# Two attention and feed-forward layers on one core: five more chunks transposed by VectorE and a trip through DRAM

## The chip, the cores and the metric

The kernel runs on one core of a Trainium2 chip. Time is device microseconds of one execution; the time of a kernel is the median of its runs. The core's engines each work through a queue of their own in the order in which the program issues their instructions: TensorE (PE in the profile; matrix multiplications and transposes, results in PSUM banks), VectorE (DVE), ScalarE (ACT), GpSimd (POOL) and SyncE (SP), whose queue issues nearly all DMA transfers. An instruction waits, with everything behind it on its engine, until what it reads has been written and what it overwrites has been read.

## The reference

`x` is 2048 rows of 448 numbers in float32. Two layers follow each other, with the same weights: attention with 16 query heads of 28 and one shared key and value head, and a gated feed-forward of width 1792, each behind a normalization of the rows and added to `x`:

```python
q = (x @ wq).reshape(B, S, H, Dh).transpose(0, 2, 1, 3)
k, v = x @ wk, x @ wv
p = softmax(einsum("bhqd,bkd->bhqk", q, k) * Dh ** -0.5)
A = einsum("bhqk,bkd->bhqd", p, v).transpose(0, 2, 1, 3).reshape(B, S, H * Dh) @ wo
B = (silu(x @ w_gate) * (x @ w_up)) @ w_down

x = x + A(layernorm(x))
x = x + B(layernorm(x))
x = x + A(layernorm(x))
x = x + B(layernorm(x))
```

## The kernel before

The 2048 rows are four chunks (0 to 3) of 512 rows, each chunk four blocks of 128 rows. `xres` holds `x` in SBUF with rows on the partitions. A product needs the chunk the other way round, with the 448 columns on the partitions (four slabs `k` of 128, the last one of 64), and as a high part `xh` and a remainder `xl`, so that three products of reduced precision stand for one of float32.

*From rows to a chunk's `xh` and `xl`.* `norm_steps` takes the statistics of four blocks (VectorE, `stats`, `mv`), the reciprocal deviation `rstd` (GpSimd) and the normalized rows `xn` (VectorE). There are two ways on from there:

- TensorE's way: `flip` (L243) issues sixteen transposes of 128x128 into PSUM banks; `flipped` lets ScalarE copy each bank to `xh` and VectorE subtract to get `xl`. GpSimd first copies the last 64 columns of `xn` once more (`twice`), so that both halves of the last slab are filled.
- VectorE's way: `turn_tile` (L266) transposes squares of 32x32 within a block, `send` (L270) stores the result to DRAM so that the squares come to lie in the right rows, a load brings it back (into `xn`, or into two of the query buffers, `qstack`), and `halved` (L286) makes `xh` and `xl` of it. The rows of the chunk then stand in another order, which later readers undo in their access patterns (`natural`, `in_order`, for the chunks listed in `squares`).

*The projection.* `Attention.project` runs sixteen products in `order`, four to a chunk; `seen` counts them, and q0 to q15 are their names in the text. Each is 11 matmuls into one PSUM bank (L312). ScalarE copies the bank out twice (L538, L539, the second into a `stage` buffer, of which the first layer has three and the second two), SyncE stores it (`qd`, and the keys `kt`), and for the two products of a chunk that hold values VectorE transposes 32 partitions (`vt`, L546). After q6, q10 and q14 four matmuls (L438, `maxima`) bound the scores of the chunk before; VectorE transposes their result (`sg`, L440), reduces it, splits it and transposes it again (`flat`), and SyncE stores it. `plan[n, 0]` and `plan[n, 1]` are lists of work issued just ahead of and just behind product n, and `when` another list behind it.

In the first layer chunks 0 to 3 all take TensorE's way: the transposes of a chunk are issued one product ahead of its first (for chunk 1, behind q3). In the second layer the last group of the feed-forward hands each chunk over as it is finished (`hand_over`): chunks 0 to 2 take VectorE's way, chunk 3 TensorE's.

*The scores* of a layer follow q15, in 128 steps that ScalarE's exponentials and TensorE fill between them. While they run, chunks 0 to 2 of the feed-forward are turned VectorE's way.

*The feed-forward* goes through seven groups of two slices of 128 columns of the 1792; a `unit` is one slice for one chunk: 42 matmuls in two halves, with the two halves of the unit before's product with `w_down` in between and behind (L332). `soon` is a list of work issued so many units later. Chunk 3 is finished last by the attention; it takes TensorE's way, its transposes issued in two blocks in the middle of the unit ahead of its first (`mid[0, 2, 1]`, the second unit of chunk 2).

The order of instructions on every engine is the order in which these functions issue them; nothing reorders it. The whole computation stands in the program a second time, with exact maxima, behind a test that doesn't ask for it on these inputs.

## Time and profile before

| | us |
|---|---|
| median of 3 runs (lowest, highest) | 1962.88 (1962.73, 1963.62) |
| the profiled execution | 1962.25 |
| its span | 1960.4 |
| TensorE matmuls, busy | 1943.3 (99%) |
| ScalarE, busy | 1264.1 (64%) |
| VectorE, busy | 968.3 (49%) |
| GpSimd, busy | 553.6 (28%) |
| first projection, first product to first scores | 12.0 to 63.7 |
| granted TensorE clock, mean | 0.998 |

Times in the views are microseconds from the start of the span. A row of a timeline is start, length, engine, line, operation, what is written from what is read, shapes and count; in brackets stands the idle time ahead of it and who ended it. A matmul's length is from its start to its result, and neighbours overlap, so what one costs is the distance between starts.

### The profile page before, as it was taken

How to read it: one execution, taken by the hardware profiler on the slowest of the kernel's cores; microseconds unless marked ns; L12 is line 12 of the kernel's file. 1: busy time of each engine (PE TensorE's matmuls, PEld its weight loads, DVE VectorE, ACT ScalarE, POOL GpSimd, SP SyncE). 2: the span in 40 equal slices, each digit the busy share in tenths (PEclk: the TensorE clock that was granted, in tenths of full speed). 3: DMA queues.
4: the chain of work that ended last, by engine and by line, in shares of the span. 5: the costliest groups of instructions: out<-in, count | busy, mean ns of one | idle time of the engine just before them, and what ended most of it. 6: DMA issues, size and time to landing. Idle time of an engine off the chain costs nothing.

```text
span 1960.4 us, 44004 instructions
## 1 busy us (share of the span) xinstructions
PE 1943.3 (99%) x18469; PEld 1325.5 (68%) x18469; DVE 968.3 (49%) x1638; ACT 1264.1 (64%) x1888; POOL 553.6 (28%) x593
## 2 busy tenths in 40 slices
PE   9999999999999999999999999999999999999998
PEld 7544545445468999999974445454454799988886
DVE  6656575665743223223666565657656433223223
ACT  4899898998943333333349998989989333333332
POOL 4213123132214333333341221121231332323320
PEclk9999999999999999999999999999999999999999
DMA  5111011121130011110251110110211200011102
GB/s 166 55 36 29 21 40 40 29 53 43 26 87 20 17 32 32 32 29 19 67 156 34 37 30 22 50 28 24 67 40 32 71 28 21 17 32 32 32 2 77
DMA packets 100643, 83.61 MB, mean 43 GB/s; under 512 B 25080, under 2 KB 81656, under 8 KB 100440
## 3 DMA queue, kind: packets, MB, share of 16 engines
q1 hardware_dynamic: 98888, 79.55, 14.7%
q8 instruction: 145, 2.38, 0.5%
q10 hardware_dynamic: 1552, 1.20, 0.2%
q14 instruction: 58, 0.48, 0.1%
HBM read 57.38 MB, written 21.50 MB: 40 GB/s over the span
## 4 chain that ended last, share of the span: by engine, by line
PE 87%; ACT 9%; DMA 1%; DVE 1%; issue 1%; POOL 0%; SPq 0%; ACTq 0%; POOLq 0%; DVEq 0%
PE bank L332 40%; PE bank L688 20%; PE bank L633 14%; ACT pt L655 6%; PE three L633 5%; PE bank L312 4%; ACT pair L656 2%; PE three L612 2%; PE bank L612 1%; PE three L621 0%; PE bank L438 0%; DMA kt<-stage 0%; DMA xd<-xh 0%; DMA wr<-in_A_wq_dram 0%; DVE vt L546 0%
## 5 line engine op out<-in xcount | busy, mean ns | idle before, releaser
L655 ACT ACTIVATE pt<-three 128x1536 f32<-128x1536 f32 x512 | 723.0, 1484 | 52.9 <-PE three L633 52.9
L688 PE MATMUL bank<-pt,vsb 128*32 128x512 f32 x3072 | 490.8, 599 | 0.0
L688 PE MATMUL bank<-pair,vsb 128*32 128x512 f32 x1024 | 487.5, 598 | 0.6 <-ACT pair L656 0.6
L633 PE MATMUL bank<-qstack,keys 32*128 32x512 f32 x1536 | 473.1, 425 | 0.0
L332 PE MATMUL bank<-xh,wgh 64*128 64x512 f32 x1728 | 450.7, 389 | 0.0
L633 PE MATMUL three<-qstack,keys 32*128 32x512 f32 x4608 | 428.7, 408 | 0.5 <-ACT stage L539 0.3
L633 PEld LDWEIGHTS bank<-qstack,keys 32*128 32x128 f32 x1536 | 243.5, 183 | 250.0 <-issue 124.9
L654 DVE COPY pair<-bank 128x512 f32<-128x512 f32 x512 | 354.0, 691 | 95.2 <-PE bank L633 57.4
L332 PE MATMUL bank<-xh,wgl 64*128 64x512 f32 x1404 | 371.7, 391 | 0.0
L332 PE MATMUL bank<-xl,wgh 64*128 64x512 f32 x1296 | 338.1, 390 | 0.0
L332 PE MATMUL bank<-wdh,h 64*128 64x448 f32 x1792 | 334.3, 364 | 1.1 <-ACT h L1008 0.8
L1007 DVE TENSOR_TENSOR sg<-bank,sg 128x512 f32<-128x512 f32 x112 | 77.4, 691 | 502.5 <-ACT sg L1006 500.3
L656 ACT ACTIVATE pair<-pair 128x1024 f32<-128x1024 f32 x256 | 281.5, 1100 | 0.0
L332 PEld LDWEIGHTS bank<-xh,wgh 64*128 64x128 f32 x1728 | 266.3, 185 | 16.7 <-issue 1.3
L633 PEld LDWEIGHTS three<-qstack,keys 32*128 32x128 f32 x4608 | 261.5, 183 | 13.9 <-DVE xres L604 1.5
L885 POOL TENSOR_TENSOR xres<-stage,xres 128x448 f32<-128x448 f32 x108 | 127.3, 1197 | 502.5 <-ACT stage L884 502.3
L688 PEld LDWEIGHTS bank<-pt,vsb 128*32 128x32 f32 x3072 | 101.9, 109 | 246.0 <-issue 153.1
L332 PEld LDWEIGHTS bank<-wdh,h 64*128 64x128 f32 x1792 | 247.5, 184 | 14.8 <-issue 2.0
L697 DVE TENSOR_TENSOR o<-bank,o 128x512 f32<-128x512 f32 x224 | 154.9, 691 | 203.8 <-PE bank L688 203.8
L339 ACT COPY seen<-bank 128x1 f32<-128x1 f32 x664 | 81.9, 163 | 254.3 <-PE bank L332 251.2
L332 PEld LDWEIGHTS bank<-xh,wgl 64*128 64x128 f32 x1404 | 219.2, 184 | 13.8
L332 PE MATMUL bank<-wdl,h 64*128 64x448 f32 x896 | 222.2, 367 | 0.0
(145 smaller groups left out, 2095.7 us busy)
## 6 DMA issues: line engine op xcount, KB each, us to landing
o<-rd SPq DMA_DIRECT2D x32, 256.0 KB
qraw<-qd SPq DMA_DIRECT2D x128, 56.0 KB
qd<-stage SPq DMA_DIRECT2D x28, 224.0 KB
wdr<-in_B_w_down_dram SPq DMA_DIRECT2D x28, 224.0 KB
xt<-tb SPq DMA_DIRECT2D x24, 224.0 KB
wr<-in_B_w_gate_dram SPq DMA_DIRECT2D x28, 192.0 KB
wr<-in_B_w_up_dram SPq DMA_DIRECT2D x28, 192.0 KB
xn<-xt SPq DMA_DIRECT2D x6, 768.0 KB
```

The lines of the kernel that those rows point to most:

```text
L312: nc.tensor.matmul(po, a, b, start=(i == 0), stop=(i == len(seq) - 1))
L332: nc.tensor.matmul(po, a, b, start=start, stop=stop, skip_group_check=True)
L339: nc.scalar.copy(seen[:, i : i + 1], po[:, 0:1])
L612: nc.tensor.matmul(po[:, 0:D], a[:, g, P * t : P * t + P], b[:, g, :], start=False, stop=(g == NG - 1 and z == 2), skip_group_check=True,)
L633: nc.tensor.matmul(three[:, j, :] if j < 3 else one, k[js, kp, ks], q[js, part, :], start=(z == 0), stop=(z == 2), tile_position=(32 * j, 0),)
L654: copies.append(nc.vector.tensor_copy(pt1, one))
L655: es.append(nc.scalar.activation(pt, threes[y], AF.Exp, scale=SCALE))
L656: es.append(nc.scalar.activation(pair, pair, AF.Exp, scale=SCALE))
L688: nc.tensor.matmul(to[32 * j : 32 * j + 32, :], vsb[:, n % NT, :], pts[n][j], start=(y == 0), stop=(y == 1), skip_group_check=True,)
L697: f = nc.vector.tensor_tensor(accs[i][:, 0, :], to, accs[i][:, 0, :], ALU.add)
L885: nc.gpsimd.tensor_tensor(r, s, r, ALU.add)
L1007: nc.vector.tensor_tensor(in_order(sg, sq), natural(pg[1], sq), in_order(sg, sq), ALU.mult)
```

## The change

Five chunks go from TensorE's way to VectorE's: chunks 2 and 3 of the first layer's projection, chunk 3 of the second layer's, and chunk 3 of both feed-forwards. Eighty of TensorE's transposes go.

- In the first layer (`by_vector`), chunk 2's statistics are issued behind q1, its normalization and transposes behind q2, its stores behind q3, its load behind q4, and its `xh` and `xl` ahead of q7; for chunk 3 these are q4, q5, q6, q8 and q11. The turned chunk goes into two tiles of half the width, so there are eight transposes of 128x224 and eight stores where other chunks have four and four. Before, statistics stood behind q4 and q8, normalization behind q5 and q9.
- In the second layer, chunk 3 is turned behind q5, stored behind q6, loaded behind q8 and split ahead of q11. Chunk 2's load moves from behind q4 to behind q3.
- In the feed-forward, chunk 3 is turned two units after the statistics, stored and loaded at once, and split by ScalarE and VectorE at the end of the unit ahead of its own first.
- In `q`, the reduction that follows a chunk's maxima (`maxima` returns it) is issued behind the product's value transpose instead of ahead of it.

```diff
     def turn_tile(got, tb, t):
-        nc.vector.transpose(tb[:, :, 32 * t : 32 * t + 32], got["x"][:, t, 0:D].rearrange("p (b w) -> p b w", w=32))
+        b0 = 0
+        for part in tb if isinstance(tb, list) else [tb]:
+            b1 = b0 + part.shape[1]
+            o = part[:, :, 32 * t : 32 * t + 32]
+            nc.vector.transpose(o, got["x"][:, t, 32 * b0 : 32 * b1].rearrange("p (b w) -> p b w", w=32))
+            b0 = b1
 
     def send(tb, raw):
         to = raw.rearrange("(b d) (g n) -> g d b n", d=32, g=4)
-        for g in range(4):
-            nc.sync.dma_start(to[g], tb[32 * g : 32 * g + 32])
+        b0 = 0
+        for part in tb if isinstance(tb, list) else [tb]:
+            b1 = b0 + part.shape[1]
+            for g in range(4):
+                nc.sync.dma_start(to[g][:, b0:b1], part[32 * g : 32 * g + 32])
+            b0 = b1
...
-            self.squares = (0, 1, 2) if layer else ()
+            self.squares = (0, 1, 2, 3) if layer else (2, 3)
...
+        def take(self, to, c):
+            if c == NC - 1:
+                raw = pers.tile([P, 4, 512], F32, name="xn")
+                rows3(raw, to)
+                return raw
+            raw = [q.bitcast(F32)[:, z, :] for q in qts[1:] for z in range(2)]
+            nc.sync.dma_start(qts[1].bitcast(F32), to[0:256, :].rearrange("(k p) n -> p k n", p=P))
+            nc.sync.dma_start(raw[2], to[256:384, :])
+            for half in (slice(0, 64), slice(64, 128)):
+                nc.sync.dma_start(raw[3][half, :], to[384:448, :])
+            return raw
...
             if not full and self.seen in (6, 10, 14):
-                self.maxima(self.seen // 4 - 1)()
+                self.late = self.maxima(self.seen // 4 - 1)
...
+            late, self.late = self.late, None
             if m > 1:
                 nc.sync.dma_start(self.kt[c][d0 : d0 + n, :], raw[112 : 112 + n, :])
+                if late:
+                    late()
                 return
...
+            if late:
+                late()
...
         def hand_over(self, c):
-            fs, got = norm_steps(c, twice=c == NC - 1)
+            fs, got = norm_steps(c, twice=False)
...
-            if c == NC - 1:
-                def ready():
-                    for f in fs[5:]:
-                        f()
-                    a.norms[c] = got
-                a.X[c] = xtile(self.xbp)
-                a.plan[5, 1] = [ready]
-                return
...
             def parts():
-                halved(a.X[c], raw, range(4), nc.scalar.copy, nc.vector.tensor_tensor)
-            self.soon.append([1, turn])
-            if c == 2:
-                a.plan[4, 1] = [load]
-                a.plan[7, 0] = [parts]
-                return
-            self.soon.append([3, parts])
-            self.soon.append([4 - c, lambda: [a.project() for _ in range(2 - c)]])
+                halved(a.X[c], got["raw"], range(4), nc.scalar.copy, nc.vector.tensor_tensor)
+            if c < 2:
+                self.soon.append([1, lambda: (turn(), store(), load())])
+                self.soon.append([3, parts])
+                self.soon.append([4 - c, lambda: [a.project() for _ in range(2 - c)]])
+            elif c == 2:
+                self.soon.append([1, lambda: (turn(), store())])
+                a.plan[3, 1], a.plan[7, 0] = [load], [parts]
+            else:
+                a.plan[5, 1], a.plan[6, 1], a.plan[8, 1], a.plan[11, 0] = [turn], [store], [load], [parts]
...
         def rest(self, xb):
-            fs3, self.norms[3] = norm_steps(3)
+            fs3, got = norm_steps(3, twice=False)
...
-            self.soon.append([1, lambda: [f() for f in fs3[5:]]])
-            self.mid[0, 2, 1] = [lambda ks=ks: self.turned(3, ks) for ks in ((0, 1), (2, 3))]
+            def turn():
+                for f in fs3[5:]:
+                    f()
+                for t in range(4):
+                    turn_tile(got, tb, t)
+                self.raw[3] = dram.tile([D, 512], F32, name=f"xt{self.layer}_3")
+                send(tb, self.raw[3])
+                self.fetch(3)
+            self.soon.append([1, turn])
+            self.soon.append([3, lambda: self.parts(3, nc.scalar.copy, nc.vector.tensor_tensor)])
...
-    for c in range(1, NC):
-        fs, got = norm_steps(c)
-        n = 4 * c - 4
-        at.plan[n, 1] = fs[:5]
-        at.plan[n + 1, 1] = fs[5:] + [lambda c=c, got=got: at.norms.__setitem__(c, got)]
+    fs, got = norm_steps(1)
+    at.plan[0, 1] = fs[:5]
+    at.plan[1, 1] = fs[5:] + [lambda got=got: at.norms.__setitem__(1, got)]
+    def by_vector(c, n0, n1, n2):
+        fs, got = norm_steps(c, twice=False)
+        to = dram.tile([D, 512], F32, name=f"xt_{c}")
+        def turn():
+            for f in fs[5:]:
+                f()
+            got["tb"] = [
+                halves("turned").bitcast(F32).rearrange("p a (b n) -> p (a b) n", n=P)[:, 0 : D // 64, :] for _ in range(2)
+            ]
+            for t in range(4):
+                turn_tile(got, got["tb"], t)
+        def parts():
+            halved(at.X[c], got["raw"], range(4), nc.scalar.copy, nc.vector.tensor_tensor)
...
+        extend((n0, 1), fs[:5])
+        extend((n0 + 1, 1), [turn])
+        extend((n0 + 2, 1), [lambda: send(got["tb"], to)])
+        extend((n1, 1), [lambda: got.__setitem__("raw", at.take(to, c))])
+        extend((n2, 0), [parts])
+    by_vector(2, 1, 4, 7)
+    by_vector(3, 4, 8, 11)
```

VectorE in the first projection, from chunk 1's normalization (`xn<-xres`) to chunk 1's first remainder (`xl`); `vt` are the value transposes of q2 and q3. Before:

```order
25 L230 TENSOR_SCALAR xn<-xres,mv,rstd 128x448 x4
26 L546 STREAM_TRANSPOSE vt<-bank_85 32x512
27 L546 STREAM_TRANSPOSE vt<-bank_86 32x512
28 L255 TENSOR_TENSOR xl<-bank_87,xh 128x512
29 L255 TENSOR_TENSOR xl<-bank_88,xh 128x512
30 L255 TENSOR_TENSOR xl<-bank_78,xh 128x512
31 L264 TENSOR_TENSOR xh<-bank_79,xh 64x512
32 L409 TENSOR_TENSOR kdiag<-few,mask 112x512
33 L217 BN_STATS stats<-xres 128x6
```

After, with the last of chunk 2's four pairs of statistics:

```order
32 L217 BN_STATS stats<-xres 128x6
33 L218 BN_AGGR mv<-stats 128x2
34 L571 STREAM_TRANSPOSE vt<-bank_85 32x512
35 L230 TENSOR_SCALAR xn<-xres,mv,rstd 128x448 x4
36 L272 STREAM_TRANSPOSE turned<-xn 128x7x32 x8
37 L571 STREAM_TRANSPOSE vt<-bank_86 32x512
38 L255 TENSOR_TENSOR xl<-bank_87,xh 128x512
```

Chunk 2's statistics, normalization (row 35) and eight transposes (row 36) now stand ahead of chunk 1's remainders (row 38), where they followed them.

ScalarE in the first feed-forward, in the unit ahead of chunk 3's first (`sg` and `h` are that unit's result, `seen` small reads that pace the engines). Before:

```order
486 L254 CAST xh<-bank_6436 128x512
487 L254 CAST xh<-bank_6437 128x512
488 L339 COPY seen<-bank_6439 128x1
489 L339 COPY seen<-bank_6440 128x1
490 L339 COPY seen<-bank_78 128x1
491 L339 COPY seen<-bank_79 128x1
492 L254 CAST xh<-bank_6436 128x512
493 L261 CAST xh<-bank_6437 64x512
494 L262 CAST xd_6623<-bank_6437 64x512
495 L1006 ACTIVATE sg<-bank_6438 128x512
496 L1008 CAST h_6994<-sg 128x512
```

After:

```order
487 L1014 ACTIVATE sg<-bank_6444 128x512
488 L1016 CAST h_6986<-sg 128x512
489 L301 CAST xh<-xn 128x512 x3
490 L308 CAST xd_6629<-xn 64x512
491 L309 CAST xh<-xn 64x512
492 L348 COPY seen<-bank_6442 128x1
```

Chunk 3's copies stood in the middle of the unit, ahead of its `sg`; they now stand behind its `h`, directly ahead of chunk 3's first unit (row 492), and read the loaded `xn`.

VectorE in the second layer's projection, from chunk 3's normalization to chunk 2's remainders (`sg` to `flat` is the maxima's chain, `vt` the value transpose of q6). Before:

```order
843 L230 TENSOR_SCALAR xn<-xres,mv,rstd 128x448 x4
844 L440 STREAM_TRANSPOSE sg<-bank_6439 128x512
845 L444 TENSOR_REDUCE ng<-sg 128x64
846 L448 CAST two<-ng 128x4x16
847 L449 TENSOR_TENSOR two<-ng,two 128x4x16
848 L451 STREAM_TRANSPOSE flat<-two 128x128
849 L546 STREAM_TRANSPOSE vt<-bank_6437 32x512
850 L293 TENSOR_TENSOR xl<-qstack_101,xh 128x512 x2
```

After:

```order
841 L230 TENSOR_SCALAR xn<-xres,mv,rstd 128x448 x4
842 L272 STREAM_TRANSPOSE xh<-xn 128x14x32 x4
843 L462 STREAM_TRANSPOSE sg<-bank_6445 128x512
844 L571 STREAM_TRANSPOSE vt<-bank_6443 32x512
845 L466 TENSOR_REDUCE ng<-sg 128x64
846 L470 CAST two<-ng 128x4x16
847 L471 TENSOR_TENSOR two<-ng,two 128x4x16
848 L473 STREAM_TRANSPOSE flat<-two 128x128
849 L302 TENSOR_TENSOR xl<-qstack_101,xh 128x512 x2
```

Four transposes of chunk 3 came in at row 842 (into a free `xh` tile), and the value transpose moved from behind the maxima's chain into it.

## The prediction

> **What bounds the kernel.** I read the page's first and fourth parts, then the timelines of TensorE (PE), VectorE (DVE), ScalarE (ACT) and SyncE's queue (SPq) around every place where the change removes transposes. Of the page, the span and the chain that ended last:

> ```profile
> span 1960.4 us, 44004 instructions
> ...
> PE 87%; ACT 9%; DMA 1%; DVE 1%; issue 1%; POOL 0%; SPq 0%; ACTq 0%; POOLq 0%; DVEq 0%
> ```

> TensorE carries 87% of the chain and whole projections and feed-forwards, so there a TensorE instruction taken away is worth its spacing, and a TensorE wait added costs its whole length. The profiled execution took 1962.25 us (its span and 1.85 around it), 0.6 below the median of 1962.88; the sum is made against 1962.25. A measurement of this kernel tells about 0.2% (4 us) from no change.

> The first projection on TensorE (start, length; L438 are the maxima of a chunk, L248 the transposes, L312 the sixteen products, which I call q0 to q15, four to a chunk):

> ```profile
> 25.43 0.50 PE L312 MATMUL bank<-xh,wh 128*128 128x512 f32 x1
> 26.42 0.51 PE L312 MATMUL bank<-xl,wh 128*128 128x512 f32 x1 [0.49 <-DVE xl L255]
> ...
> 33.89 1.10 PE L438 MATMUL bank<-q,kdiag 112*128 112x512 f32 x4
> 34.83 2.08 PE L248 MATMUL bank<-ident,xn 128*128 128x128 f32 x16
> 36.66 0.48 PE L312 MATMUL bank<-xh,wh 128*128 128x512 f32 x1
> ...
> 39.50 0.39 PE L312 MATMUL bank<-xl,wh 128*128 128x512 f32 x1
> ...
> 46.76 1.10 PE L438 MATMUL bank<-q,kdiag 112*128 112x512 f32 x4
> ...
> 52.67 0.50 PE L312 MATMUL bank<-xl,wh 128*128 128x512 f32 x1
> ```

> The rows at 26.42, 39.50 and 52.67 are the second matmuls of q4, q8 and q12, the first that read a new chunk's low part xl, which VectorE writes. VectorE there:

> ```profile
> 20.34 1.78 DVE L230 TENSOR_SCALAR xn<-xres,mv,rstd 128x448 f32<-128x448 f32 x4 [1.42 <-POOL rstd L223]
> ...
> 25.68 1.89 DVE L255 TENSOR_TENSOR xl<-bank,xh 128x512 fp32r<-128x512 f32 x3
> ...
> 28.93 0.62 DVE L217 BATCH_NORM_STATS2 stats<-xres 128x6 f32<-128x448 f32 x1
> ...
> 33.43 1.78 DVE L230 TENSOR_SCALAR xn<-xres,mv,rstd 128x448 f32<-128x448 f32 x4 [1.49 <-POOL rstd L223]
> 35.24 0.72 DVE L440 STREAM_TRANSPOSE sg<-bank 128x512 f32<-128x512 f32 x1
> ...
> 37.63 0.72 DVE L546 STREAM_TRANSPOSE vt<-bank 32x512 f32<-32x512 f32 x1
> 38.38 1.89 DVE L255 TENSOR_TENSOR xl<-bank,xh 128x512 fp32r<-128x512 f32 x3
> ```

> TensorE already waits 0.49 us for VectorE at 26.42. VectorE is half idle over the kernel, but not here, and it works in the order written.

> **What the change removes.** Five chunks lose sixteen TensorE transposes each. A group is spaced 36.66 - 34.83 = 1.83 us, and 5 x 1.83 = 9.2 us is the most that this can give.

> **First projection, chunk 1.** Nothing of chunk 1 itself changes, but chunk 2's statistics, normalization and eight VectorE transposes now stand on VectorE ahead of chunk 1's xl. I rebuild the queue from the rows. Chunk 1's normalization ends at 20.34 + 1.78 = 22.12 as before. Chunk 2's statistics with the wait for rstd take 33.43 - 28.93 = 4.50 (to 26.6; the value transpose of q2 fits into that wait), its normalization 35.24 - 33.43 = 1.81 (to 28.4). Then come eight transposes of 128x224, a shape that before doesn't have. The nearest rows, by form and in a timeline:

> ```profile
> L268 DVE STREAM_TRANSPOSE xh<-xn 128x448 f32<-128x448 f32 x12 | 6.6, 610 | 0.0
> ...
> L451 DVE STREAM_TRANSPOSE flat<-two 128x128 f32<-128x128 f32 x8 | 2.5, 312 | 0.3
> ```

> ```profile
> 970.45 2.22 DVE L268 STREAM_TRANSPOSE xh<-xn 128x448 f32<-128x448 f32 x4
> ```

> Four of 128x448 are 0.54 apart, so eight halves take between 8 x 0.27 = 2.1 (no fixed part) and 8 x 0.54 = 4.3 (nothing but a fixed part). By the two lengths, 610 ns at 448 and 312 at 128, a half is 400 ns, less the 70 ns by which neighbours overlap: 0.33 apart, 2.65 for eight. That I take (to 31.1). The value transpose of q3 adds 38.38 - 37.63 = 0.75 (31.85). From the first xl on VectorE to TensorE passed 26.42 - 25.68 = 0.74, so TensorE goes on at 32.6 instead of 26.42: 6.2 us late, after standing idle since about 25.9. Nothing hides this: q4 to q15 are all queued behind that one matmul.

> **Chunk 2.** From xl to the next statistics VectorE needs 28.93 - 25.68 = 3.25 (35.1), then chunk 3's 4.50, 1.81 and 2.65 (44.05), then chunk 1's maxima chain with one value transpose, 38.38 - 35.24 = 3.14 in either order (47.2), then 0.74: chunk 2's xl reaches TensorE at 47.95. TensorE is ready earlier: 32.6 + (33.89 - 26.42) + 0.94 for the maxima + (39.50 - 36.66) for q7 = 43.85. It waits 4.1 us more, and q8 stands at 47.95 against 39.50: 8.45 late, transposes already saved.

> **Chunk 3.** The maxima of chunk 2 start 46.76 - 39.50 = 7.26 later, at 55.2. Two paths now lead to q12. By VectorE: 55.2 + 1.21 (maxima to sg, rows at 1015.83 and 1017.04 below) + 3.14 + 0.74 = 60.3. By memory, with these rows of the second layer's trip and of a load from DRAM, SPq and POOL:

> ```profile
> 972.69 3.01 SPq L274 DMA_DIRECT2D xt<-xh  x4
> ...
> 978.85 0.38 SPq L934 DMA_DIRECT2D qstack<-xt  x1
> ```

> ```profile
> 301.47 0.44 SPq L130 DMA_DIRECT2D xn<-xt  x1
> ```

> ```profile
> 306.78 0.61 POOL L292 CAST xh<-xn 128x512 fp32r<-128x512 f32 x1 [1.81 <-DMA xn<-xt]
> ```

> Four sends are issued in 3.01, the load follows 978.85 - 975.70 = 3.15 after the last one, and the first reader starts 306.78 - 301.47 = 5.31 after the load's issue. Eight half-size sends carry the same bytes with twice the instructions: 3.0 to 6.0, I take 4.0, nearer to equal bytes. Chunk 3's sends stand on SyncE behind the store of chunk 1's maxima (flat), which VectorE finishes at 47.2, so: 47.6 + 4.0 + 3.15 + 5.31 + 1.39 (ACT's copy to TensorE's xl, 1005.43 to 1006.82 below) = 61.45. Against 52.67 that is +8.8.

> **The clock.** The trace has one long wait of TensorE in a dense stretch, at chunk 2 of the second layer's projection:

> ```profile
> 1006.10 0.50 PE L312 MATMUL bank<-xh,wh 128*128 128x512 f32 x1 [1.72 <-ACT xh L292]
> 1006.82 0.50 PE L312 MATMUL bank<-xl,wh 128*128 128x512 f32 x1 [0.22 <-DVE xl L293]
> ...
> 1015.83 1.10 PE L438 MATMUL bank<-q,kdiag 112*128 112x512 f32 x4
> ...
> 1018.43 0.48 PE L312 MATMUL bank<-xh,wh 128*128 128x512 f32 x1
> ...
> 1021.29 0.39 PE L312 MATMUL bank<-xl,wh 128*128 128x512 f32 x1
> ```

> ```profile
> 1008.00:1014.00 6.00, 6.00 (x21) 4.77 (x20) 1.47 (x3) 2.61 (x6) 3.57 (x8) 0.75 0.45 143
> ```

> The second fence is a window after it: the column 0.75 is the granted clock, which loses 6 x 0.25 = 1.5 us. A wait of 1.72 was enough. So I charge 1.5 wherever a wait is longer than that. Chunk 1's loss is swallowed by chunk 2's wait. Chunk 2's loss moves the maxima to 56.7 and VectorE's path to 61.8, past memory's; q12's wait is then 61.8 - (56.7 + 0.94 + 2.84) = 1.3 and costs none. First projection: 61.8 - 52.67 = **+9.1**.

> [...]

> **Feed-forward, last chunk, both layers.**

> ```profile
> 606.85 1.09 PE L248 MATMUL bank<-ident,xn 128*128 128x128 f32 x8
> 607.88 0.47 PE L332 MATMUL bank<-wdh,h 64*128 64x448 f32 x2
> ...
> 613.97 0.84 PE L332 MATMUL bank<-xh,wgh 64*128 64x512 f32 x2
> 614.33 0.72 PE L332 MATMUL bank<-xl,wgh 64*128 64x512 f32 x2
> ```

> ```profile
> 598.54 1.77 DVE L230 TENSOR_SCALAR xn<-xres,mv,rstd 128x448 f32<-128x448 f32 x4
> ```

> Two blocks of eight go from the unit ahead of chunk 3's first, 607.88 - 606.85 = 1.03 each, so TensorE reaches chunk 3 at 613.97 - 2.06 = 611.9. The data now takes the trip: normalized at 600.3, turned at 602.5 (2.22), sent at 605.55 (3.01), landed at 608.7 (3.15), loaded for ACT at 614.0 (5.31), xl on TensorE 1.39 later at 615.4. Before it was 614.33: +1.1, and the idle stretch before the first xh is 614.7 - 611.9 = 2.8, longer than 1.72: 1.5 of clock. **+2.6 in each layer, +5.2**.

> **Second layer's projection.** VectorE and ScalarE there:

> ```profile
> 1002.91 0.71 DVE L440 STREAM_TRANSPOSE sg<-bank 128x512 f32<-128x512 f32 x1
> ...
> 1006.08 1.98 DVE L293 TENSOR_TENSOR xl<-qstack,xh 128x512 fp32r<-128x512 f32 x3
> ...
> 1017.04 0.72 DVE L440 STREAM_TRANSPOSE sg<-bank 128x512 f32<-128x512 f32 x1 [4.17 <-PE bank L438]
> ```

> ```profile
> 1005.43 1.88 ACT L292 CAST xh<-qstack 128x512 fp32r<-128x512 f32 x3 [2.27 <-DMA qstack<-xt]
> ```

> Chunk 2's load is issued one product earlier, so memory no longer ends the wait at 1006.10. VectorE does: chunk 3's four transposes (spaced 4 x 0.54 = 2.15) come ahead of sg, and the 1006.08 - 1002.91 = 3.17 up to xl follow unchanged. TensorE's q8 goes on at about 1008.95 instead of 1006.82, +2.1; the clock loss is there already. The maxima then start at 1017.95, and chunk 3's xl comes 1.21 + 3.17 + 0.74 later, at 1023.05, against 1021.29: **+1.7**, after a wait of 1023.05 - (1017.95 + 0.94 + 2.84) = 1.3, no clock. Memory is earlier there (sent from 1008.2: 3.01 + 3.15 + 5.31 + 1.39 gives 1021.1).

> **Costed at nothing.** ScalarE's four copies and VectorE's four subtractions per chunk stay and only read another source. GpSimd loses its copies of xn, off the path. Loads of turned data stop SyncE's queue until the sends have landed, and the product stores, value and key loads behind them go out some 3 us late; the cover is that scores read them only after q15, and that TensorE has eight banks. If a staging buffer ran out, ScalarE would stop, then TensorE. In the second layer there are two staging buffers, and q4's store is now behind the loads: ScalarE's copies for chunk 2 may come no earlier for it, but VectorE ends that wait.

> **Sum.** 9.1 + 5.2 + 1.7 = +16.0; 1962.25 + 16.0 = 1978.

> **Rivals.**
> - The clock stays up after the two feed-forward waits: -3.0, 1975. For it: the only wait with a loss was followed by a second of 0.22, and nothing else long is in the trace. Against it: 1.72 was enough. [...]
> - Only the first projection is hurt. If the feed-forward's and second layer's xl come in time, these places gain 2 x 2.06 + 1.83 = 5.95: 1962.25 + 9.1 - 5.95 = 1965. It would need the feed-forward's trip of 13.7 us (600.3 to 614.0) to be over 3 us shorter, for which no row speaks.
> - Faster: VectorE gets chunk 1's xl out in time, so that TensorE only loses transposes, 1962.25 - 9.2 = 1953. It decides at 26.42: the work put ahead of xl would have to fit into VectorE's idle time between 22.12 and 25.68, less one value transpose. That is under 3 us for 4.50 + 1.81 + 2.65 = 9. I see no way.
> - Dearer: transposes at 0.54, sends at 6.0. Each of two rounds of transposes adds 1.65, the sends 2.0, and memory ends q12's wait at 61.45 + 5.3 = 66.75, +14.1, with a clock loss of 1.5 there; two longer feed-forward trips of 1 us and a second clock loss of 1.5 in the second layer make +26: 1988.

> **Numbers.** Forecast as summed, 1976.5 to 1982: 0.45. Clock stays up, or the cheap ends of transposes (-0.5 a round) and sends (-1.0), 1970 to 1976.5: 0.25. Dearer, above 1982: 0.20. Only the first projection hurt, about 1965: 0.06, of which most lies within 4 us of before. Faster: 0.04. Range 1970 to 1988: it takes in the first three cases but for the rim of the dear one. Faster 0.04, same 0.05, slower 0.91.

> **What would show it.** In the timeline of the changed kernel TensorE's second matmul of q4 near 32.6 with a wait of some 6 us put down to VectorE's xl, of q8 near 48, of q12 near 61 to 62; half-width transposes 0.33 apart; in the feed-forward an idle stretch near 612 to 615 that ends with ScalarE's xh and memory ahead of it; granted clock below 1 in the windows after each. Wrong would make it: VectorE's eight transposes much cheaper, a trip through memory several us shorter, or q4 running before 27 us.

## The result, and the profile after

The changed kernel takes 1987.72 us (median of 4 runs, 1984.87 to 1988.85) against 1963.2 for the kernel before: a ratio of 1.0123, 95% interval 1.0105 to 1.0140. That is +24.5 us where +16.0 was forecast. The sign held, and the sum was too small by 8.5 us. The range of 1970 to 1988 held by 0.3 us only, in the case above 1982 that had a chance of 0.20.

Two lines of the changed kernel's page:

```profile
span 1985.9 us, 43921 instructions
...
PE 1943.0 (98%) x18389; PEld 1273.5 (64%) x18389; DVE 980.8 (49%) x1666; ACT 1258.9 (63%) x1888; POOL 545.3 (27%) x573
```

TensorE's busy time is that of before (1943.3), although up to 9.2 us of transposes are gone, so other matmuls took longer (parts of them ran at a granted clock of 0.50, as shown below); and it stands idle for 1985.9 - 1943.0 = 42.9 us instead of 17.1.

Where the time came in is read from the start of the same instruction in both traces: the second matmul of q0, the first of each layer's scores, and a matmul that reads `xd` in a unit some 20 us behind chunk 3's first in each feed-forward (their units repeat every 7.29 us, so the same one is found by its distance). A column is the stretch between two such marks, and a cell is how much longer it is than before, in us, one profiled execution each. The rows under `changed` are the experiments of the next section:

| kernel | up to q0 | 1st projection | 1st feed-forward | 2nd projection | 2nd feed-forward | span |
|---|---|---|---|---|---|---|
| forecast | 0 | 9.1 | 2.6 | 1.7 | 2.6 | 16.0 |
| changed | 0.4 | 11.7 | 3.6 | 5.1 | 4.9 | 25.5 |
| e1_first | 2.0 | 12.6 | 0.0 | 0.9 | 0.3 | 16.6 |
| e2_ff | 0.3 | 0.0 | 0.6 | 0.2 | 2.3 | 3.9 |
| e3_second | 1.8 | 0.0 | -0.1 | 8.0 | 0.7 | 10.8 |
| e4_late | 0.2 | -0.4 | 0.2 | 0.1 | -0.1 | -0.2 |
| e5_fill | 0.2 | 12.4 | 1.2 | 6.3 | 0.5 | 20.0 |
| e6_load | 0.2 | 10.8 | 1.8 | 7.6 | 4.7 | 24.9 |
| e7_chain | 0.3 | 12.2 | 3.5 | 6.8 | 4.0 | 26.5 |
| e8_order | 0.7 | 13.5 | 1.7 | 5.6 | 4.2 | 25.2 |
| e9_early | 0.4 | 0.0 | -1.1 | 0.1 | -0.9 | -1.6 |
| e10_sends | 0.6 | 11.4 | 4.0 | 8.8 | 3.0 | 27.9 |
| e11_all | 0.6 | 9.5 | -0.9 | 9.2 | -0.8 | 17.6 |
| e12_queue | 0.5 | 14.0 | 3.9 | 9.5 | 5.4 | 33.0 |

A cell is good to about 2 us: e12_queue has the changed kernel's first projection and differs by 2.3 there, e6_load its first feed-forward and differs by 1.8, and e3_second, which changes nothing ahead of the second projection, has 1.8 in the first column. By the last section one stretch at half clock makes a step of some 1.6 us.

**First projection.** TensorE's timeline of the changed kernel:

```profile
32.42 0.79 PE L321 MATMUL bank<-xl,wh 128*128 128x512 f32 x1 [5.85 <-DVE xl L255]
...
47.33 0.50 PE L321 MATMUL bank<-xl,wh 128*128 128x512 f32 x1 [2.19 <-DVE xl L302]
...
54.83 1.10 PE L460 MATMUL bank<-q,kdiag 112*128 112x512 f32 x4
...
62.86 0.77 PE L321 MATMUL bank<-xh,wh 128*128 128x512 f32 x1 [4.42 <-ACT xh L301]
```

q4 and q8 came where they were forecast (32.6 and 47.95). q12 did not: its xl follows at about 63.6 instead of 61.8, and the wait is put down to ScalarE's xh, which waits for memory, and not to VectorE. SyncE's queue (SPq), and ScalarE's reader of the loaded chunk:

```profile
47.44 0.34 SPq L475 DMA_DIRECT2D rows<-flat  x1
47.84 4.32 SPq L282 DMA_DIRECT2D xt<-turned  x8
...
55.81 0.40 SPq L130 DMA_DIRECT2D xn<-xt  x1
```

```profile
62.19 1.66 ACT L301 CAST xh<-xn 128x512 fp32r<-128x512 f32 x3 [5.61 <-DMA xn<-xt]
```

The sends start at 47.84 (forecast 47.6) and take 4.32 (4.0). The load follows 3.65 after the last one (3.15), and its reader 6.38 after the load (5.31). The clock also fell in another place. A row of the next view is a stretch of time: its start and end, its length, how long TensorE was busy in it (and with how many matmuls), the granted clock, the DMA engines' share and GB/s:

```profile
42.43:45.85 3.42, 2.71 (x12) 1.00 0.84 243
45.85:49.26 3.41, 1.93 (x8) 1.00 0.52 156
...
62.91:66.33 3.42, 3.42 (x8) 0.50 0.51 152
```

The wait of 5.85 at q4 cost clock (0.50 from 28.8 to 35.6), but q8 waits for VectorE behind it, so that this is hidden, as forecast. The wait of 2.19 at q8 cost none (1.00 in both rows around it), so TensorE came to q12 early and waited 4.42 there, which did (0.50 from 62.91). From q12's xl to the first scores it took 12.22 us instead of 11.04.

**Feed-forward**, first layer: TensorE, SyncE, ScalarE, and TensorE's clock around the wait.

```profile
627.33 0.79 PE L341 MATMUL bank<-xh,wgh 64*128 64x512 f32 x2 [3.46 <-ACT xh L301]
628.05 0.79 PE L341 MATMUL bank<-xl,wgh 64*128 64x512 f32 x2
```

```profile
614.64 3.23 SPq L282 DMA_DIRECT2D xt<-tb  x4
...
621.13 0.39 SPq L130 DMA_DIRECT2D xn<-xt  x1
```

```profile
626.66 1.66 ACT L301 CAST xh<-xn 128x512 fp32r<-128x512 f32 x3 [2.01 <-DMA xn<-xt]
```

```profile
622.70:626.11 3.41, 1.16 (x11) 1.00 0.90 294
626.11:629.53 3.42, 2.20 (x10) 0.50 1.11 229
629.53:632.94 3.41, 3.41 (x20) 0.50 0.00 1
```

Less the 12.1 us by which the layer runs late, xl stands at 615.95 (forecast 615.4). From the first send to the reader the trip took 626.66 - 614.64 = 12.0 us, near the forecast (3.01 + 3.15 + 5.31 = 11.5). The clock is at half for 6.83 us; the row from before on which the forecast rests had lost 1.5.

**Second projection**: TensorE, SyncE, ScalarE and VectorE, in this order.

```profile
1018.28 1.10 PE L460 MATMUL bank<-q,kdiag 112*128 112x512 f32 x4
...
1024.43 0.49 PE L321 MATMUL bank<-xh,wh 128*128 128x512 f32 x1 [2.54 <-ACT xh L301]
1026.88 0.79 PE L321 MATMUL bank<-xl,wh 128*128 128x512 f32 x1 [1.95 <-DVE xl L302]
...
1041.95 0.50 PE L321 MATMUL bank<-xh,wh 128*128 128x512 f32 x1 [1.52 <-ACT xh L301]
```

```profile
1016.27 0.38 SPq L391 DMA_DIRECT2D qstack<-xt  x1
...
1018.98 0.40 SPq L566 DMA_DIRECT2D kt<-stage  x1
...
1026.41 0.34 SPq L475 DMA_DIRECT2D rows<-flat  x1
1026.80 3.11 SPq L282 DMA_DIRECT2D xt<-xh  x4
...
1034.78 0.39 SPq L130 DMA_DIRECT2D xn<-xt  x1
```

```profile
1023.28 0.58 ACT L561 COPY stage<-bank 128x512 f32<-128x512 f32 x1 [3.73 <-DMA kt<-stage]
...
1041.28 1.66 ACT L301 CAST xh<-xn 128x512 fp32r<-128x512 f32 x3 [2.72 <-DMA xn<-xt]
```

```profile
1023.89 0.72 DVE L571 STREAM_TRANSPOSE vt<-bank 32x512 f32<-32x512 f32 x1 [1.83 <-ACT stage L561]
...
1026.17 2.27 DVE L302 TENSOR_TENSOR xl<-qstack,xh 128x512 fp32r<-128x512 f32 x3
```

Two staging buffers hold q4 and q5. q4's key store now stands behind chunk 2's load, goes out at 1018.98 and has landed 4.2 later; until then ScalarE cannot copy q6, and q8's xh is queued behind that copy. VectorE's value transpose waits for the same copy, and the maxima's chain, now behind it, and chunk 2's xl wait too: 8.60 us from the maxima to q8's xl. Chunk 3 had been turned at 1021.46, but its sends stand on SyncE behind the chain's `flat`: 1026.80.

### The profile page after: what moved, and what is told of

The parts are those of the page before. It is cut to its first block, busy times and chain, and to the rows that moved or that the text cites. A ratio compares the mean times of both kernels' runs of the same rounds, so it can differ in the third digit from the quotient of the medians.

```text
span 1985.9 us, 43921 instructions
## 1 busy us (share of the span) xinstructions
PE 1943.0 (98%) x18389; PEld 1273.5 (64%) x18389; DVE 980.8 (49%) x1666; ACT 1258.9 (63%) x1888; POOL 545.3 (27%) x573
## 3 DMA queue, kind: packets, MB, share of 16 engines
q1 hardware_dynamic: 111112, 89.38, 16.6%
## 4 chain that ended last, share of the span: by engine, by line
PE 42%; ACT 5%; DMA 2%; DVE 1%; SPq 1%; issue 0%; POOL 0%; DVEq 0%; ACTq 0%; POOLq 0%
PE bank L341 20%; PE bank L715 10%; PE bank L660 7%; ACT pt L682 3%; PE three L660 2%; PE bank L321 1%; ACT pair L683 1%; PE three L639 1%; DMA xn<-xt 1%; DMA xt<-xh 0%; PE bank L639 0%; DMA xt<-tb 0%; DVE xn L230 0%; SPq L282 0%; PE three L648 0%
## 5 line engine op out<-in xcount | busy, mean ns | idle before, releaser
L341 PE MATMUL bank<-xh,wgh 64*128 64x512 f32 x1728 | 356.9, 391 | 8.2 <-ACT xh L301 7.9
L341 PE MATMUL bank<-xh,wgl 64*128 64x512 f32 x1404 | 310.2, 393 | 0.0
L341 PE MATMUL bank<-wdh,h 64*128 64x448 f32 x1792 | 300.5, 364 | 1.2 <-ACT h L1016 0.8
L660 PEld LDWEIGHTS three<-qstack,keys 32*128 32x128 f32 x4608 | 261.9, 183 | 13.5 <-DVE xres L631 1.5
L341 PE MATMUL bank<-xl,wgh 64*128 64x512 f32 x1296 | 268.1, 392 | 0.0
L348 ACT COPY seen<-bank 128x1 f32<-128x1 f32 x664 | 76.7, 164 | 267.2 <-PE bank L341 265.6
L1014 ACT ACTIVATE sg<-bank 128x512 f32<-128x512 f32 x112 | 67.2, 600 | 212.6 <-PE bank L341 212.6
L341 PEld LDWEIGHTS bank<-xh,wgh 64*128 64x128 f32 x1728 | 176.1, 186 | 39.2 <-ACT xh L301 8.6
L341 PEld LDWEIGHTS bank<-wdh,h 64*128 64x128 f32 x1792 | 180.4, 184 | 21.3 <-issue 1.7
L341 PE MATMUL bank<-wdl,h 64*128 64x448 f32 x896 | 175.8, 367 | 0.0
```

What stands on the lines that cost most here:

```text
L341: nc.tensor.matmul(po, a, b, start=start, stop=stop, skip_group_check=True)
L348: nc.scalar.copy(seen[:, i : i + 1], po[:, 0:1])
L660: nc.tensor.matmul(three[:, j, :] if j < 3 else one, k[js, kp, ks], q[js, part, :], start=(z == 0), stop=(z == 2), tile_position=(32 * j, 0),)
L1014: nc.scalar.activation(in_order(sg, True), natural(pg[0], True), AF.Silu)
```

## The experiments

Times are medians beside the kernel before on the same chip, with the ratio and its 95% interval.

**Each part alone.** On the kernel before: the first projection's part (e1), the feed-forwards' (e2), the second projection's without the chain's move (e3), and only that move (e4). The fences of this section show the lines of an edit that matter, not all of it.

```diff
 e1  + by_vector(2, 1, 4, 7)
     + by_vector(3, 4, 8, 11)
 e2  - self.mid[0, 2, 1] = [lambda ks=ks: self.turned(3, ks) for ks in ((0, 1), (2, 3))]
     + self.soon.append([1, turn])
     + self.soon.append([3, lambda: self.parts(3, nc.scalar.copy, nc.vector.tensor_tensor)])
 e3  + a.plan[3, 1], a.plan[7, 0] = [load], [parts]
     + a.plan[5, 1], a.plan[6, 1], a.plan[8, 1], a.plan[11, 0] = [turn], [store], [load], [parts]
 e4  - self.maxima(self.seen // 4 - 1)()
     + self.late = self.maxima(self.seen // 4 - 1)
```

> The kernel before with only the first projection's part (chunks 2 and 3 of layer 0 by VectorE and memory; the maxima's chain stays ahead of the values). By the trace of the changed kernel, in which the first scores start 75.81 - 63.71 = 12.1 us later, the parts add: +12.1 us, 1975. By the prediction's own step +9.1, 1972. The rival, that the three parts hurt each other (a late start of layer 0 that makes later waits longer), would give clearly less than 12 here and less than 24.5 for the three parts together.

> The kernel before with only the feed-forwards' last chunk by VectorE and memory. By the marks in the changed kernel's trace (one row behind chunk 3's first units stands 15.73 - 12.10 = 3.6 later in layer 0 and 25.78 - 20.88 = 4.9 in layer 1, of which a little may be the scores'): +8.0, 1971. By the prediction's step +5.2, 1968. If the waits there only show because of what went before: about 0.

> The kernel before with only the second layer's projection changed: chunk 3 by VectorE and memory, chunk 2's load one product earlier, the maxima's chain still ahead of the values. The changed kernel lost 20.88 - 15.73 = 5.2 there. If ScalarE's copy of q6 into a staging buffer, held until q4's store has gone out behind the load, is the cause by way of ScalarE's own queue, most of it stays: +4 to +5, 1967. If it works by way of the value transpose that now stands ahead of the chain (and waits for that copy), the chain is free here: +2 to +3, 1965. By the prediction's step +1.7, 1964.6.

> The kernel before with only the maxima's chain moved behind the value transpose, in both layers. In the trace of before the staging copy of q6 ends at 1003.16, ahead of the end of sg at 1003.62, so the value transpose would not wait: 0.0 us, 1962.9. The rival, that the value transpose waits for ScalarE wherever it stands first, gives up to +2 in each layer.

Measured against 1962.44: e1 1976.98, ratio 1.0070 (1.0054 to 1.0087); e2 1968.40, 1.0028 (1.0017 to 1.0040); e3 1970.90, 1.0038 (1.0025 to 1.0051); e4 1962.52, 1.0003 (0.9993 to 1.0013). The four ratios less one add up to 1.39% against 1.23% for the whole, within the intervals: by the medians the parts add, three of them slow the kernel, and the chain's move alone costs nothing that these runs can tell. Place by place the traces agree less well: e2's feed-forwards lost 2.9 in its trace and the changed kernel's 8.5, e3's second projection 8.0 and the changed kernel's 5.1. e3's median is above all three of its forecasts. It lost that time with the chain ahead of the values, so the chain's place is not what makes that part dear.

**The idle time filled.**

```diff
+ fill(24)      # 24 transposes of ident into a LOW bank, ahead of chunk 3's first unit
```

> The changed kernel with 24 transposes of the identity (128x128, results read by nobody) issued on TensorE just ahead of chunk 3's first feed-forward unit, in both layers, where it stands idle for 3.46 us. They take 24 x 0.114 = 2.7 us of that wait and nothing else. If the clock falls because TensorE stands idle, the granted clock stays near 1 behind it and each layer gets back about 2 us: -4, 1983.7. If the wait is all that costs, or the clock falls anyway: 0, 1987.7; if the transposes run past the end of the wait, up to +1.

Measured 1983.67 against 1963.20, ratio 1.0108 (1.0091 to 1.0124), 4 us under the changed kernel's median. TensorE and the window around the end of the wait, first layer:

```profile
624.43 2.84 PE L868 MATMUL bank<-ident 128*128 128x128 f32 x24
627.62 0.49 PE L341 MATMUL bank<-xh,wgh 64*128 64x512 f32 x2 [0.35 <-ACT xh L301]
```

```profile
626.92:630.33 3.41, 2.83 (x24) 1.00 0.85 199
```

Data come no earlier, but the clock stays at 1.00 where it was 0.50, and the feed-forwards lose 1.2 and 0.5 instead of 3.6 and 4.9. The idle stretch, by way of the clock, is most of what they cost.

**Second projection: the load, and the chain.** The changed kernel with chunk 2's load back behind q4 (e6), and with the chain back ahead of the value transpose (e7).

```diff
 e6  - a.plan[3, 1], a.plan[7, 0] = [load], [parts]
     + a.plan[4, 1], a.plan[7, 0] = [load], [parts]
 e7  - self.late = self.maxima(self.seen // 4 - 1)
     + self.maxima(self.seen // 4 - 1)()
```

> The changed kernel with chunk 2's load in the second layer's projection put back behind q4 and its stores. If q4's store behind the load is what holds the staging buffer, ScalarE's copy of q6 is free some 2 us earlier (its store issued at 1016.9 instead of 1018.98), the load some 1 us later, and xl of chunk 2 reaches TensorE at about 1024.6 instead of 1026.88: -2.3, with less clock lost up to -3.8: 1984 to 1985.5. If the chain and VectorE's order alone set it: 0, 1987.7.

> The changed kernel with the maxima's chain back ahead of the value transpose, in both layers. If the value transpose's wait for ScalarE (1.83 us) is what sets chunk 2 in the second layer, the chain runs from 1022.1, xl starts at 1024.6 instead of 1026.17: -1.5, with less clock lost up to -2.5: 1985 to 1986. If ScalarE's own queue sets it (xh starts at 1023.76 in any order): 0 to -0.7. The first layer: 0, since flat is stored some 0.75 earlier and sends start at most that much earlier.

Measured against 1963.20: e6 1987.60, ratio 1.0127 (1.0110 to 1.0144); e7 1988.42, 1.0130 (1.0113 to 1.0147). Neither gained. TensorE in e6:

```profile
1015.56 1.10 PE L460 MATMUL bank<-q,kdiag 112*128 112x512 f32 x4
...
1022.35 0.80 PE L321 MATMUL bank<-xl,wh 128*128 128x512 f32 x1 [1.54 <-DVE xl L302]
...
1039.10 0.79 PE L321 MATMUL bank<-xh,wh 128*128 128x512 f32 x1 [2.63 <-ACT xh L301]
```

q8's xl now follows the maxima by 6.79 instead of 8.60, so the held staging buffer was the cause there. But q12 waits 2.63 instead of 1.52, and the clock, which falls behind q8 in both kernels (0.50 from 1025.47 to 1032.30 in the changed kernel; matmuls 0.43 us apart instead of 0.23 behind q8 in both), falls behind q12 as well here (granted 0.57 from 1038 to 1042, against 1.00 in the changed kernel): what q8 gains, q12 gives back. e7 gains 1.4 at q8 (its xl stands at 1025.98, its maxima at 1018.82, 7.16 apart) and loses it again: its q12 waits 3.29.

**First projection: chunk 2's work behind chunk 1's xl.**

```diff
- extend((n0 + 1, 1), [turn])
+ extend((n0 + (2 if c == 2 else 1), 1), [turn])
```

> The changed kernel with chunk 2's normalization and transposes in the first projection put behind chunk 1's xl (its statistics stay ahead of it). If VectorE's work ahead of chunk 1's xl were the whole loss, q4 comes some 5.4 us earlier and the kernel gains that: 1982. If q8 is set by chunk 2's trip, which hardly moves (xl ends 29.2, turned 33.5, sent 38, landed 41.1, read 46.4), q8 stays at 47.5 and the wait of q4 moves to q8, 9 us long, with a clock loss behind it; q12 then comes without a wait, since chunk 3's trip keeps its place: -3, 1984.7, the gain all at q12. If q12's trip moves with it: 0.

Measured 1985.67 against 1963.20, ratio 1.0111 (1.0094 to 1.0128): no difference to the changed kernel that these runs can tell. TensorE:

```profile
27.94 0.50 PE L321 MATMUL bank<-xl,wh 128*128 128x512 f32 x1 [1.25 <-DVE xl L255]
...
43.94 0.80 PE L321 MATMUL bank<-xh,wh 128*128 128x512 f32 x1 [4.90 <-ACT xh L301]
46.88 0.80 PE L321 MATMUL bank<-xl,wh 128*128 128x512 f32 x1 [2.15 <-DVE xl L302]
```

q4's wait of 5.85 is down to 1.25, and q8 stands within 0.8 us of where it stood (33.4 behind q0 instead of 34.2). Taking VectorE's queue away ahead of q4 only moves the wait to q8. My further guess, that q12 would gain, fell: it waited 4.57.

**Chunk 3's sends ahead of the queue.**

```diff
- extend((n0 + 2, 1), [lambda: send(got["tb"], to)])
+ extend((n0 + (1 if c == 3 else 2), 1), [lambda: send(got["tb"], to)])
- by_vector(3, 4, 8, 11)
+ by_vector(3, 4, 7, 11)
- a.plan[5, 1], a.plan[6, 1], a.plan[8, 1], a.plan[11, 0] = [turn], [store], [load], [parts]
+ a.plan[5, 1], a.plan[7, 1], a.plan[11, 0] = [turn, store], [load], [parts]
```

> The changed kernel with chunk 3's four (eight) sends issued right behind its transposes in both projections, ahead of q6's stores and of the store of the maxima (flat), and its load one product earlier. In the changed kernel SyncE's queue held the sends from 43.58 (turned) to 47.84 in the first layer and from 1021.46 to 1026.80 in the second. If that order sets q12, the first layer's chunk 3 is sent by 47.9, landed 51.1, read at 57.2 to 57.7, and TensorE, ready at 58.44, waits no more: -4.4 of wait and -1.7 of clock there; the second layer's wait of 1.52 goes too: -7, 1980.5. If the load's own trip sets it (6.4 us, wherever it starts, because other transfers slow it): -2 to -4. If VectorE or the stores now held back on SyncE (q6's, and with them ScalarE's staging buffers) set it: 0 or more.

Measured 1986.66 against 1962.91, ratio 1.0118 (1.0101 to 1.0135): no gain. SyncE in the first layer, ScalarE in both:

```profile
44.77 5.95 SPq L282 DMA_DIRECT2D xt<-turned  x8
...
53.04 0.38 SPq L130 DMA_DIRECT2D xn<-xt  x1
```

```profile
60.67 1.66 ACT L301 CAST xh<-xn 128x512 fp32r<-128x512 f32 x3 [3.43 <-DMA xn<-xt]
...
1040.33 0.59 ACT L561 COPY stage<-bank 128x512 f32<-128x512 f32 x1 [1.83 <-DMA kt<-stage]
```

Sends that start 3.1 us earlier bring the data only 1.5 earlier: they take 5.95 instead of 4.32, and the reader starts 7.63 after the load instead of 6.38. In the second layer the load, now ahead of q8's stores, holds a staging buffer just as chunk 2's load did, this time under q10. That place went from 5.1 to 8.8; the clock is at half there from 1043.1 to 1050.0, which it is not behind q12 of the changed kernel.

**Stores on another queue.** The changed kernel, with the second layer's product stores issued by ScalarE.

```diff
- nc.sync.dma_start(self.qd[c][112 * m : 112 * m + 112, :], raw[0:112, :])
+ out = nc.scalar if self.layer else nc.sync
+ out.dma_start(self.qd[c][112 * m : 112 * m + 112, :], raw[0:112, :])
```

> The changed kernel with the second layer's product stores (qd and kt) issued by ScalarE's own queue, behind the staging copy they belong to, instead of SyncE's, where they stand behind loads that wait for their sends. If SyncE's order is what holds the two staging buffers, q4's store goes out at about 1016.7 instead of 1018.98 and lands 4.2 later, ScalarE's copy of q6 comes at 1021 instead of 1023.28, xl of chunk 2 reaches TensorE 2 us earlier, the chain's flat and with it chunk 3's sends follow 2 us earlier, so that q12 keeps that gain: -2 to -5 (the clock), 1983 to 1986. If the landing of the stores alone holds the buffers (two are too few in any order), or the issues cost ScalarE as much: 0, 1987.7. If q12 gives the gain back, as with chunk 2's later load: 0.

Measured 1995.14 against 1962.49, ratio 1.0156 (1.0142 to 1.0170): slower still, which none of the cases foresaw. TensorE and SyncE:

```profile
1021.21 1.10 PE L460 MATMUL bank<-q,kdiag 112*128 112x512 f32 x4
...
1027.33 0.50 PE L321 MATMUL bank<-xl,wh 128*128 128x512 f32 x1 [2.28 <-DVE xl L302]
...
1046.78 0.80 PE L321 MATMUL bank<-xh,wh 128*128 128x512 f32 x1 [6.77 <-ACT xh L301]
```

```profile
1027.64 5.43 SPq L282 DMA_DIRECT2D xt<-xh  x4
...
1035.30 3.39 SPq L443 DMA_DIRECT2D qraw<-qd  x4
1038.79 0.39 SPq L130 DMA_DIRECT2D xn<-xt  x1
```

No staging copy of that projection waits for a store any more, and q8's xl follows the maxima by 6.12 instead of 8.60. But q12 now waits 6.77: the sends take 5.43, and the load stands behind `qraw`'s, which wait for products to be stored. So chunk 3's way through memory bounds that projection, and the held buffer was only the first of two limits.

**The feed-forward's trip one unit earlier**, on e2: chunk 3's normalized rows in a tile of their own, turned behind the first unit.

```diff
- fs3, got = norm_steps(3, twice=False)
+ fs3, got = norm_steps(3, p3, twice=False)     # p3: a pool that is open for the first group
- self.soon.append([1, turn])
- self.soon.append([3, lambda: self.parts(3, nc.scalar.copy, nc.vector.tensor_tensor)])
+ self.soon.append([0, turn])
+ self.soon.append([2, lower])                  # slabs 0, 1 by GpSimd
+ self.soon.append([3, lambda: half((2, 3), nc.scalar.copy, nc.vector.tensor_tensor)])
```

> The kernel before with only the feed-forwards' part, and the trip of chunk 3 started one unit earlier: its normalized rows get a tile of their own (so that VectorE need not wait until GpSimd has read chunk 2's), normalized and turned behind the first unit, GpSimd makes xh and xl of slabs 0 and 1 one unit early, ScalarE and VectorE those of slabs 2 and 3 as before. In the changed kernel's times VectorE is free from 604.3 to 608.7, so turned at 608.3, sent 611.5, landed 614.8, read 620.3, xl of slab 0 at 622.2 by GpSimd, and TensorE reaches chunk 3 at 623.9. If the trip's late start is the whole loss, each layer saves the 2.06 us of transposes less at most 0.7 of wait for slab 2: -3 to -4, 1959 to 1960, faster than the kernel before. If the trip through memory costs TensorE by itself (loads that meet the weights' on SyncE's queue, ScalarE's copies late for the units around it): 0 to +4.

Measured 1962.89 against 1961.73, ratio 1.0006 (0.9997 to 1.0015): no faster. In the trace each feed-forward gains about 1 us (the waits are 0.85 for GpSimd's xl and 0.18 for VectorE's in the first layer, 1.28 for GpSimd's in the second), but that execution was the shortest of eleven, and the median shows none of it. Against e2's 1.0028 the edit removes the loss. The earlier start came with the new tile and with GpSimd's half, and no run parts the three; together they don't turn the part into a gain.

**All three mends** (e6, e9, e10) together:

> The changed kernel with three edits together: chunk 3's sends right behind its transposes and its load one product earlier (both projections), chunk 2's load in the second layer back behind q4's stores, and the feed-forwards' trip one unit earlier with a tile of its own and GpSimd's half. If the places are independent: -7, -2 to -4 (the clock behind q8 and q12 of the second layer included) and -3.6 - 4.9 - 2.0 = -10.5 for the feed-forwards, 1987.7 - 20 = 1967. What stays then is the first projection's q4 and q8. If a gain at one wait is given back at the next, as with the load alone: 1975.

Measured 1979.78 against 1962.91, ratio 1.0087 (1.0070 to 1.0104), above both forecasts. The feed-forwards were mended (-0.9 and -0.8), the first projection perhaps a little (9.5), the second projection not at all (9.2): the feed-forwards keep their gain whatever the projections do, but within a projection the limits follow one another. No kernel here beats the one before.

## Why the prediction was right and wrong

- *The loss sits where VectorE's and memory's way is longer than TensorE's slack: right.* All four places lost time. q4 and q8 of the first projection came within 0.7 us of the forecast, and half transposes are 0.30 apart (0.33).
- *q12 of the first projection: wrong in who ends it, and by 2.6 us.* The step "60.3 by VectorE, 61.45 by memory" had the memory path as a sum of quiet durations. The same path took 14.35 us from first send to reader instead of 4.0 + 3.15 + 5.31 = 12.5. In the feed-forwards, forecast at 11.5, it took 12.0 and 13.0 (11.1 and 11.6 in e2); in the projections' traces, for this chunk, 12.8 (e1) to 18.5 (e12). What in it is other transfers' load on the DMA engines and what the queue's order was not separated. Of the 2.6 us, 1.4 are q12's later xl and 1.2 the half clock behind it.
- *"So I charge 1.5 wherever a wait is longer than that": wrong as a rule.* The clock stayed at 1.00 after 2.19 at q8 and fell to 0.50 at q12, after 4.42. For the changed kernel's feed-forwards the charge of 1.5 was too small: the filled idle time brought back 2.4 and 4.4 there in the traces, and 4.05 together by the medians, where 3.0 was charged. With the feed-forwards' part alone (e2) the clock fell to 0.50 behind one of the two waits in the trace (rows below), and the medians lost 6.0 where 5.2 was forecast.
- *Second projection, +1.7: wrong, 5.1.* The step that failed stands under "Costed at nothing": with two staging buffers and q4's store behind the load, ScalarE's copies "may come no earlier for it, but VectorE ends that wait". ScalarE stood idle for 3.73 ahead of its copy of q6, VectorE itself waited for that copy, and so did the sends of chunk 3. Less the 15.7 us by which that projection runs late, q8's xl came 4.3 later than before instead of 2.1. "Memory is earlier there (sent from 1008.2)" failed with it: sends stood behind `flat` for 5.3 us, and at q12 it was memory that ended the wait.
- *The dear rival's time (1988) came out, its prices not.* Memory did end q12's wait with a loss of clock behind it, as that rival had it. But transposes cost 0.30, not 0.54, and sends 4.3, not 6.0. By the table the sum missed 0.4 at the start, 2.6 and 3.4 in the projections, 1.0 and 2.3 in the feed-forwards, from queues and from the clock. That the total fell inside the range is luck.

## What to carry to other kernels

Before a trip through memory is put into a stretch that already stores and loads on the same queue, follow that queue in order: whatever stands behind a load that waits for its own stores holds its buffer, and the buffer's writer, for as long (q4's key store held ScalarE's copy of q6 for 3.73 us here). Price such a trip from rows of the busy stretch and not of a quiet one (14.35 us against 12.5), and look for the second limit before mending the first, since a wait that is taken away ahead of an unchanged late arrival only moves to it (in e8 q4's wait went from 5.85 to 1.25, and q8 stayed within 0.8 us of its place). A wait can cost clock behind it as well, as q12's of 4.42 did here (0.50) and q8's of 2.19 did not (1.00): look at the granted clock behind each wait, and not at the wait alone.

## What the runs showed of the hardware

```profile
1004.21:1007.63 3.42, 1.47 (x6) 1.00 0.79 242
1007.63:1011.04 3.41, 3.41 (x10) 0.50 0.49 160
```

In e2 TensorE waited 2.55 us ahead of chunk 3 in the first layer and 3.07 in the second. The first wait was cut in two by the edge of a stretch (1.82 and 2.23 busy), and the clock was 1.00 in both; of the second, TensorE was idle for 3.41 - 1.39 = 2.02 in one stretch, and the next one, to 1589.91, was at 0.50:

```profile
610.29:613.70 3.41, 1.82 (x17) 1.00 0.89 291
613.70:617.11 3.41, 2.23 (x16) 1.00 1.10 232
...
1583.09:1586.50 3.41, 1.39 (x10) 1.00 1.14 203
```

The 2.19 us at q8 of the changed kernel were cut in two as well (2.71 and 1.93 busy). In the traces of before and of the changed kernel, without the first 16 and the last 25 us, six stretches at 1.00 were followed by one at 0.50, and in each of the six TensorE had been idle for 1.95 us or more; the other 1114 at 1.00 had at most 1.61. Of the ten stretches at 0.50, the four in which TensorE was idle for 0.66 us or more were followed by another one at 0.50, and the six with 0.23 or less by one at 1.00. The four stand behind the waits at q4, in both feed-forwards and at q8 of the second layer's projection, all in the changed kernel, which lost two stretches in a row there.

What a stretch at 0.50 costs shows in the spacing of the changed kernel's matmuls: behind q12's wait the 128x512 ones are 0.43 us apart from 64.17 to 66.31 and 0.23 from 66.56. A fully busy stretch of 3.41 us so costs about 3.41 x (1 - 0.23 / 0.43) = 1.6 us, an estimate from these two spacings. Counted from the start of the span, the edges lie at 0.70 us and whole multiples of 3.413 behind it in the kernel before, at 1.47 in the changed kernel. I take it that whether a wait of 2 to 3 us costs clock is therefore partly luck; no run shows it on one and the same kernel. Of e2's seven executions the profiled one was the shortest (1966.08, clock 0.998; the others 1967.66 to 1970.01 at 0.995 to 0.997).

In e9 VectorE's normalization of chunk 3 took twice as long as in the kernel before. It ran while GpSimd copied and subtracted on 512 columns; four instructions took 3.78 instead of the 1.77 and 1.78 of the timelines quoted for the kernel before:

```profile
592.16 3.78 DVE L230 TENSOR_SCALAR xn<-xres,mv,rstd 128x448 f32<-128x448 f32 x4
...
594.38 1.31 POOL L311 TENSOR_TENSOR xh<-xn,xd 64x512 fp32r<-64x512 f32 x1
```

In the changed kernel the same four, started at 610.70 when GpSimd had nothing to do, took 1.78; but at 20.34 in the kernel before they took 1.78 too, beside GpSimd's copies of 64 columns (1.44 for four, from 20.99). So they were not longer beside every GpSimd instruction, and no run shows why they were in e9.
